# Naming the PSUM bank of each feed-forward tile and re-ordering a fused attention and feed-forward kernel

## The chip, the cores and the metric

The kernel runs on one core of one Trainium2 chip. The metric is the device time of one execution in microseconds. The kernel before has a median of 408.99 us over three runs (408.08, 413.05 and 408.99).

Five engines take part. TensorE (PE) multiplies matrices and writes only to PSUM, an accumulator memory of eight banks. VectorE (DVE) and ScalarE (ACT) read PSUM and write SBUF, the working memory. GpSimd (POOL) works in SBUF and issues some DMA transfers. SyncE (SP) issues most transfers. Each engine takes its own instructions strictly in the order in which the program emits them, and engines wait for one another through semaphores.

## The reference

Eight batches of eight heads attend over 576 positions of 64 values, with a decay between positions that comes from a running sum of the logarithm of `f`. The result, 4608 tokens of 512 values, goes through a feed-forward layer with two input matrices that are multiplied element by element.

```python
scores = scale * np.matmul(q, k.transpose(0, 1, 3, 2))
cum = np.cumsum(np.log(np.clip(f, 0.0001, 1.0)), axis=-1)
decay = cum[:, :, :, None] - cum[:, :, None, :]
scores = np.where(causal, -1000000000.0, scores + decay)
attn = softmax(scores)                       # with 1e-09 added to the sum
x = np.matmul(attn, v)  -> reshaped to (4608, 512)
out = ((x @ w_a) * (x @ w_b)) @ w_out        # w_a, w_b: 512 x 1536; w_out: 1536 x 512
```

## The kernel before

Attention works on 32 steps t, each a pair of heads of one batch (four steps to a batch). One step goes through these operations; their names are those of the planner and are used below.

- `pt` transposes a quarter of a batch's queries or keys on TensorE into a PSUM tile `psT`; `pe` evicts that on ACT or DVE.
- `qk t.g` computes the scores of one group g of query blocks into a PSUM tile `sc` of two banks; there are two such tiles. Group 0 is the pair of blocks 0 and 1. From batch 1 on, the `max` operations on DVE add the decay from the table `spread`, write the sum to SBUF, and find the row maximum (`do_decay`, L575). In batch 0 the decay is added on TensorE.
- `exp` on ACT (L602, L606), a reciprocal on DVE (L614, L616), `norm` on POOL (L624).
- `tr` transposes the probabilities by DMA on SP's queue; the early steps use TensorE instead (`ptr`, L74) and evict with `pev`.
- `pv` multiplies the probabilities by the values (L666, L682); `ev` copies the result to the layer's input `xT`.

From batch 2 on, `pv` of step t-2 is emitted with step t. Its last part, `do_pv4` for the 64 queries left over, writes to columns 448 to 511 of the first bank of step t's group 0 score tile, which the scores leave unused ("spare"). So two unrelated values share a bank: the scores of step t, which DVE reads four times (`max t.0` and `max t.1`, two heads each), and the older step's output, which L693 reads.

The feed-forward layer takes tokens in pieces of 256, 256, 256, 384 and then 512. For each piece and each of twelve blocks of the hidden dimension, TensorE makes `psa` and `psb` (eight matmuls each), ACT copies `psa` (`acopy`), DVE multiplies it by `psb` (`mul`, L964), and three groups of eight matmuls per 128 tokens make `pso`, which ACT or DVE copies out (`ocopy`) and SP stores. This layer's work is spread between the attention steps, so that TensorE has something to do while DVE, ACT and POOL work on the softmax; a last part remains when attention is done.

Six kinds of PSUM tile share three banks under the tag "ff": `psT`, `scd` (which spreads the decay table), `psP` (of `ptr`), `psa`, `psb` and `pso`. The tile pool of the program gives each new tile one of the three (`bufs=3`), as they come free in the order of emission. There are 396 such tiles.

The emission order is fixed: each piece of work is an `Op` with an engine, a duration, the operations that it depends on, and the buffers it takes. A planner outside the kernel uses these to look for an order; the kernel holds its answer, a list of 2460 operation numbers (`ORDER`), and a letter for each operation that may run on several engines (`CHOICE`, 103 letters). `laid_out` reads both, and the operations are emitted in that order. The framework adds the semaphore waits that the emitted order needs: a reader waits for the writers emitted before it, and a writer for the readers emitted before it.

Of the kernel before, what the change touches and what calls it, by code (L numbers as in the profile page):

```python
# [25 lines left out]
def kernel(  # L26
# [111 lines left out]
    ps = pool("ps", 1, space=bass.MemoryType.PSUM)  # L138
    VEC = {"ACT": nc.scalar, "DVE": nc.vector, "POOL": nc.gpsimd}
# [29 lines left out]
    T = {}  # L169
# [132 lines left out]
    def pe_transpose(b, which, half):  # L302

        x = T[("n16", which, b, half)]
        x = x if b in EARLY else x.rearrange("p t h d -> p t (h d)")
        p = [ps.tile([128, 1024], FP16, tag="ff", bufs=3, name="psT") for _ in range(2)]
        for t in range(TG):
            for j in range(2 if b in EARLY else 1):
                for m, r in enumerate(HP):
                    nc.tensor.matmul(out=p[m][HP[j] if b in EARLY else slice(0, 128), 64 * t:64 * t + 64],  # L310
                                     lhsT=x[r, j, t, :] if b in EARLY else x[r, t, :], rhs=ident16[r, r],
                                     is_transpose=True, start=(t == 0), stop=(t == TG - 1), skip_group_check=True)
        for m in range(2):
            T[("psT", which, b, 2 * half + m)] = p[m]
# [201 lines left out]
    def spread_mm(t, h):  # L516
        c = T[("scd", t, h)] = ps.tile([128, 512], FP32, tag="ff", bufs=3, name="scd")
# [122 lines left out]
    def pe_tr(t, part, lo, hi):  # L640
        src = PB[t % RING["PB"]] if part == "B" else T[("P", part[0], t)]
        p = ps.tile([128, 8, 128], FP16, tag="ff", bufs=3, name="psP")
# [70 lines left out]
    def attention(t, base):  # L713
# [36 lines left out]
        qk_of, sc_of = {}, {}  # L750
        qk_prev = None
        for gs in ([(0,), (1,), (2, 3)] if b in EARLY else [(0,), (1,), (2,), (3,)]):
# [30 lines left out]
            if gs == (0,) and b not in EARLY and old // NP not in EARLY:  # L783
# [166 lines left out]
    def ff_mm(t0, n, fb, w16, name):  # L950
        p = ps.tile([128, 512], FP32, tag="ff", bufs=3, name=name)
# [16 lines left out]
    def ff_out(t0, tb, part):  # L968
        if part == 0:
            T[("pso", t0, tb)] = ps.tile([128, 512], FP32, tag="ff", bufs=3, name="pso")  # L970
# [98 lines left out]
    for n in cuts:  # L1069
# [3 lines left out]
        0-2 45 49 53 28-31 36 32 37-39 33 35 41 34 4-9 46 10 47 50 43 51 52 11 57 3 78 54 56 65 63 61 42  # L1073
# [5 lines left out]
        101 106 23 24 162 244 163 245 207 387 263 208 252 125 264 265 107 253 102 388 144 1750-1752 150  # L1079
# [15 lines left out]
        461 460 379 448 1827 1831 455 443 1832-1834 1836 1838 465 466 1835 472 1802 512 498 514 377 429  # L1095
        1807 467 1837 517 1840-1842 432 1844 473 1839 1843 468 1845 474 1846 1848 521 433 1849 499 449
        513 515 564 456 522 462-464 450 524 380 1850 1852 520 523 1847 529 469 530 470 381 475 543 544
# [7 lines left out]
        606 621 620 589 485 694-696 608 486 1902 1904 1903 1906 627 1907 1908 632 633 1905 578 705 585  # L1105
# [10 lines left out]
        759 904-906 798 772 813 1977-1979 749 717 735 908 820 742 766 801 769 802 1980 811 761 760 821  # L1116
        793 804 803 741 787 788 795 912 914 856 857 1976 1982 817 909 1983 1984 910 823 835 836 828 805
        807 806 915 799 911 822 1987 819 838 830 837 839 842 843 1988 1985 1989 1991 1992 824 1993 1990
        829 1994 841 794 800 812 840 763 762 1981 1995 818 916 814 831 825 779-781 832 928 827 834 929
# [5 lines left out]
        934 921 935 936 2029 924 923 933 962 922 949 2031-2033 2035 2036 2030 953 2034 954 1112 1020  # L1125
# [113 lines left out]
```

## Time and profile before

| quantity | value |
|---|---|
| median of three runs | 408.99 us (408.08 to 413.05) |
| the profiled execution | 408.72 us, of which the span from first to last instruction is 407.0 us |
| TensorE busy | 392.3 us (96% of the span), 5792 matmuls |
| VectorE busy | 303.6 us (75%) |
| ScalarE busy | 280.1 us (69%) |
| GpSimd busy | 263.0 us (65%) |
| mean granted TensorE clock | 0.996 |

The busy time of an engine is the time in which at least one of its instructions was running. A row of a timeline has the start and the length of an instruction or of a merged run of like instructions, with "xN" for their count, and in brackets the idle time of the engine before it and the event that ended that idle time. A row of the waits names who waited for whom, the total in microseconds, how often, and the longest. Idle time of an engine that does not set the pace costs nothing by itself.

### The profile page before, as it was taken

Reading aid. Unit: us, or ns where it says so; the run is one execution under the profiler, and the core shown is the slowest. Engines: PE = TensorE matmul, PEld = TensorE weight load, DVE = VectorE, ACT = ScalarE, POOL = GpSimd, SP = SyncE. Lnnn points to the kernel's source line nnn. Section 1 sums busy time; section 2 is a strip of 40 time slices with the busy share of each in tenths; the row PEclk is TensorE's granted clock in tenths of the full one; section 3 lists DMA queues with packets and bytes.
Section 4 is the critical chain, followed back from the end, with each engine's and each line's share of the span. In section 5 each row is a group of like instructions: output and inputs, shape, how many; then the busy total and the mean of one; then the engine's idle time right before and its main releaser. Section 6 shows DMA issues by size and latency. Waiting matters only on the chain. (4 is left out here: it accounts for less than half of the span.)

```text
span 407.0 us, 14850 instructions
## 1 busy us (share of the span) xinstructions
PE 392.3 (96%) x5792; PEld 246.9 (61%) x5792; DVE 303.6 (75%) x1012; ACT 280.1 (69%) x793; POOL 263.0 (65%) x488
## 2 busy tenths in 40 slices
PE   7899799999999999999999899999999999999995
PEld 2557586877966655555556456555555555556783
DVE  4888788999898888977896989679878884432331
ACT  4698799979986688787785678488676882231230
POOL 8898569868888588686987774778975493000000
PEclk9899999999999999999999999999999999999999
DMA  7999996999999999999999989999998569100202
GB/s 127 188 208 161 183 217 158 216 282 209 270 266 215 222 228 235 262 254 216 259 212 271 260 194 240 234 262 256 192 199 187 111 137 183 53 2 22 86 2 77
DMA packets 147190, 76.88 MB, mean 189 GB/s; under 512 B 124336, under 2 KB 129200, under 8 KB 147120
## 3 DMA queue, kind: packets, MB, share of 16 engines
q1 hardware_dynamic: 141040, 68.73, 75.3%
q0 software_dynamic: 5936, 7.08, 10.8%
q8 instruction: 45, 0.74, 0.7%
q14 instruction: 25, 0.20, 0.2%
q10 hardware_dynamic: 144, 0.13, 0.1%
HBM read 52.05 MB, written 9.58 MB: 151 GB/s over the span
## 5 line engine op out<-in xcount | busy, mean ns | idle before, releaser
L575 DVE CUSTOM_DVE_ANT_0 S<-sc,spread 64x576 f32<-64x576 f32 (+4 forms) x232 | 125.8, 562 | 11.3 <-PE sc L682 3.2
L74 PE MATMUL psb<-xT,wb 128*64 128x512 f16 (+2 forms) x1056 | 117.4, 341 | 1.4 <-DMA wb<-in_moe_w_b_dram 1.0
L74 PE MATMUL psa<-xT,wa 128*64 128x512 f16 (+2 forms) x1056 | 117.4, 341 | 0.4 <-issue 0.2
L624 POOL TENSOR_SCALAR PA<-PA,st 128x256 f16<-128x256 f16 (+2 forms) x192 | 90.2, 480 | 35.0 <-DVE st L616 23.6
L258 ACT CAST a<-psa 128x512 f16<-128x512 f32 (+2 forms) x132 | 66.6, 505 | 62.0 <-PE psa L74 54.0
L964 DVE TENSOR_TENSOR ht<-psb,a 128x512 f16<-128x512 f32 (+2 forms) x132 | 77.4, 590 | 33.5 <-PE psb L74 29.0
L74 PE MATMUL pso<-wout,ht 128*64 128x512 f16 x864 | 101.4, 380 | 0.0
L606 ACT ACTIVATE PA<-S,st 128x256 f16<-128x256 f32 (+2 forms) x168 | 84.3, 504 | 13.3 <-DVE st L575 12.9
L624 POOL TENSOR_SCALAR PB<-PB,st 128x512 f16<-128x512 f16 (+1 forms) x96 | 67.6, 712 | 18.6 <-DVE st L616 4.6
L74 PEld LDWEIGHTS <-wb 128*64 128x64 f16 x1056 | 60.3, 110 | 31.6 <-issue 3.4
L74 PEld LDWEIGHTS <-wa 128*64 128x64 f16 x1056 | 60.1, 110 | 31.2 <-issue 2.5
L74 PEld LDWEIGHTS <-ht 128*64 128x64 f16 x864 | 48.8, 110 | 35.4 <-issue 1.3
L606 ACT ACTIVATE PB<-S,st 128x512 f16<-128x512 f32 x56 | 40.2, 720 | 4.1 <-DVE st L575 3.5
L452 PE MATMUL sc<-kT,qT 64*128 64x128 f16 (+3 forms) x384 | 34.1, 267 | 1.3 <-ACT qT L256 0.4
L606 ACT ACTIVATION_READ_ACCUMULATOR PA<-S,st 128x1 f32 x168 | 32.0, 190 | 0.0
L262 DVE CAST xT<-pv 128x512 f16<-128x512 f32 (+1 forms) x40 | 23.1, 577 | 6.4 <-PE pv L666 6.2
L262 DVE COPY osb<-pso 128x512 f32<-128x512 f32 x17 | 11.7, 689 | 19.9 <-PE pso L74 19.8
L452 PEld LDWEIGHTS <-qT 64*128 64x128 f16 (+1 forms) x384 | 13.2, 95 | 21.7 <-issue 14.5
L666 PEld LDWEIGHTS <-nv 128*64 128x64 f16 x640 | 22.4, 110 | 6.5 <-issue 1.3
L602 ACT ACTIVATE PB<-S,st 128x576 f16<-128x576 f32 x28 | 21.8, 778 | 5.9 <-POOL PA L624 2.3
L575 DVE CUSTOM_DVE_ANT_1 S<-sc,spread 128x256 f32<-128x256 f32 x48 | 19.8, 418 | 7.7 <-PE sc L682 2.4
L258 ACT COPY osb<-pso 128x512 f32<-128x512 f32 x18 | 10.4, 580 | 20.7 <-DMA out_dram<-osb 10.8
(101 smaller groups left out, 480.9 us busy)
## 6 DMA issues: line engine op xcount, KB each, us to landing
spread<-cum_d SPq DMA_DIRECT2D x24, 576.0 KB, 5.8
out_dram<-osb SPq DMA_DIRECT2D x35, 256.0 KB, 3.5
v<-in_v_dram SPq DMA_DIRECT2D x32, 256.0 KB, 5.3
q<-in_q_dram SPq DMA_DIRECT2D x12, 576.0 KB, 6.0
k<-in_k_dram SPq DMA_DIRECT2D x12, 576.0 KB, 6.5
wout<-in_moe_w_out_dram POOLq DMA_DIRECT2D x3, 512.0 KB, 7.6
v<-in_v_dram SPq DMA_DIRECT2D x8, 128.0 KB, 3.7
wb<-in_moe_w_b_dram POOLq DMA_DIRECT2D x2, 512.0 KB, 9.9
```

Of the source, the lines that this page charges most:

```text
L74: nc.tensor.matmul(out=out[r], lhsT=lhsT[:, r], rhs=rhs, **kw)
L258: nc.scalar.copy(out=out_, in_=in_)
L262: VEC[e].tensor_copy(out=out_, in_=in_)
L452: nc.tensor.matmul(out=dst, lhsT=lhsT, rhs=rhs, start=start, stop=stop, skip_group_check=True)
L575: nc.vector.tensor_tensor_reduce(out=o, in0=x, in1=y, scale=-1.0, scalar=3e38, op0=ADD, op1=MIN, accum_out=m)
L602: nc.scalar.activation(out=p_blocks(t, 4), in_=T[("s" if direct else "z", t, 4)], func=EXP, bias=st[:, 8:9], scale=sign, accum_out=st[:, 1 ...
L606: nc.scalar.activation(out=p_blocks(t, i)[:, :, h, :], in_=(T[("s", t, i)][:, h, :] if direct else T[("z", t, i)][:, h * n:h * n + n]).rea ...
L624: VEC[e].tensor_scalar(out=p, in0=p, scalar1=st[:, c:c + 1], scalar2=1.0, op0=MUL, op1=MUL)
L666: nc.tensor.matmul(out=o[HP[h], 128 * i:128 * i + 128], lhsT=vt[:, j, pr + NP * h, :], rhs=pt[:, base_blk[i] + 2 * block_at(t, i, j) + h, ...
L964: nc.vector.tensor_tensor(out=ht[:, 0:n], in0=T.pop(("psb", t0, fb))[:, 0:n], in1=T.pop(("a16", t0, fb))[:, 0:n], op=MUL)
```

## The change

Three things change in the text of the kernel.

1. The six places that took a tile from the pool of three buffers now call `ff_tile`, which takes the next digit of a table `FFBANK` (396 digits, 0 to 2) and asks for the one buffer under that tag. The tiles, their count and their contents are as before.
2. In the operations' dependencies, `pv` of step t-2 gets the four `max` operations of step t's group 0 as predecessors, so in any order that the planner finds it is emitted behind them.
3. `ORDER` and `CHOICE` are replaced by new ones.

The operations themselves, the number of matmuls (5792) and the buffers are the same.

```diff
+    ff_bank = []
+
+    def ff_tile(shape, dtype, name):
+        return ps.tile(shape, dtype, tag=f"ff{ff_bank.pop(0)}", bufs=1, name=name)
...
-        p = [ps.tile([128, 1024], FP16, tag="ff", bufs=3, name="psT") for _ in range(2)]
+        p = [ff_tile([128, 1024], FP16, "psT") for _ in range(2)]
...
-        p = ps.tile([128, 512], FP32, tag="ff", bufs=3, name=name)
+        p = ff_tile([128, 512], FP32, name)
...
-        qk_of, sc_of = {}, {}
+        qk_of, sc_of, spare_pv = {}, {}, []
...
                 sc_of[0].append(pv)
+                spare_pv.append(pv)
                 late[old][1](pv, sc_of[0])
...
+                    if g == 0 and spare_pv:
+                        spare_pv[0].deps.append(mx)
...
     ORDER = """
-        0-2 45 49 53 28-31 36 32 37-39 33 35 41 34 4-9 46 10 47 50 43 51 52 11 57 3 78 54 56 65 63 61 42
...
+        0 1 45 2 49 28 29 4-8 46 9 10 30-33 36 37 47 48 50 51 35 38 34 39 11 53 57 3 78 61 65 63 42 54
...
     CHOICE = """
-        DDPDADAADADDPADDDDDAADDADDADDDADAAAAAADDAADADADADADAADAAAAAAAADAAAAADADAAADAAADAAAAADDADDADD
-        ADAAAAAAADA
+        DDDPAAAADADAPPADADDDADDADDADDAAAAADAAADDADDDADDAADAAAAAAAAADAAAAAAAADAAAAADAAAAAAAAADAAAAADA
+        DAADAAAAADA
     """
+    FFBANK = """
+        02102101201021021021012012012012012012012012021012021021021210210210212012021021012012012012
...
     def laid_out():
+        ff_bank.extend("".join(FFBANK.split()))
```

Compared operation by operation, the new order keeps the broad course of the old one. On TensorE the steps' score groups, the feed-forward groups and the `pv` stand in nearly the same sequence from end to end; neighbours are exchanged. Before, in six of the 22 late `pv` (those of steps 8, 15, 19, 22, 26 and 27) one to three of the four readers of the shared bank were emitted behind the `pv`; after, none. On POOL the first load of keys stands ahead of the identity matrix that TensorE's first matmuls need, where it stood behind it; the last input weights (`ldwa`, `ldwb`) no longer stand behind a part of `w_out`, and the load `ldc1q1` stands ahead of the last of them. Seven evictions of transposed queries and keys move from DVE to ACT, one copy of the decay table moves from DVE to ACT, and one cast of values from DVE to POOL.

More of the change, by code (lines that the diff above doesn't have):

```diff
@@ L516, in spread_mm @@
     def spread_mm(t, h):
-        c = T[("scd", t, h)] = ps.tile([128, 512], FP32, tag="ff", bufs=3, name="scd")
+        c = T[("scd", t, h)] = ff_tile([128, 512], FP32, "scd")
         mm_halves(c, pickh[h][:, t:t + 1].to_broadcast([128, 128]), crow[:, 0:512], start=True, stop=True)
@@ L641, in pe_tr @@
         src = PB[t % RING["PB"]] if part == "B" else T[("P", part[0], t)]
-        p = ps.tile([128, 8, 128], FP16, tag="ff", bufs=3, name="psP")
+        p = ff_tile([128, 8, 128], FP16, "psP")
         for n in range(lo, hi):
@@ L969, in ff_out @@
         if part == 0:
-            T[("pso", t0, tb)] = ps.tile([128, 512], FP32, tag="ff", bufs=3, name="pso")
+            T[("pso", t0, tb)] = ff_tile([128, 512], FP32, "pso")
         o = T[("pso", t0, tb)]
@@ L1105 @@
-        606 621 620 589 485 694-696 608 486 1902 1904 1903 1906 627 1907 1908 632 633 1905 578 705 585
[10 rows of a table removed]
[L1116 to L1119, printed above, removed]
[5 rows of a table removed]
@@ L1125 @@
-        934 921 935 936 2029 924 923 933 962 922 949 2031-2033 2035 2036 2030 953 2034 954 1112 1020
[9 rows of a table removed]
-        1061 2078-2080 1080 1086 2081 1075 2083 2084 1094 1093 2085 2082 1098 1099 2086 1088 1139 1051
[4 rows of a table removed]
-        1142 1131 1146 1153 1144 1140 1143 1159 2106 1172 1187 1175 1177 1133 1194 1323 2108-2110 1160
-        1195 1197 1132 1176 1178 2111 1111 1110 2113 1191 1329 2114 1188 2107 1240 1135 1167 1203 1161
-        1179 1162 1173 1202 1154 1169 1168 1181 1196 1209 1174 1210 1204-1206 1189 1330 1331 1198 1211
[10 rows of a table removed]
@@ L1153 @@
-        1272 1275 1261 1253 1274 1292 1299 1533 1307 1317 1319 1312 1537 2172 1374 1360-1362 1367 1363
-        2173 1376 1375 1318 1404 1306 1293 1357 2176-2178 2181 1352 2182 1380 2179 1366 2174 1368 1381
[8 rows of a table removed]
-        1475 2218-2220 1499 1493 2221 2223 1544 1558 1549 1418 1463 1481 1445 2222 1511 1512 1469 1559
-        1500 1550 1476 1464 1543 1482 1471 1456 1457 1483 2224 1439 1438 2225 2227 1514 2228 1513 1507
-        1504 2226 1501 1502 1506 1494 1551 1490 2229 1552 1492 2190 1604 1556 1485 2185 1495 1515 1508
@@ L1166 @@
-        2230 1518 1519 2231 2232 1553 2233 2235-2237 1517 1516 1503 1488 1470 1484 1545 1510 1491 1523
-        1520 2234 1524 1521 2238 1525 1526 2239 2240 1561 1546 1565 2241 1527 1569 1583 1584 1548 1547
-        1571 1586 1577 1585 2242 1587 1570 1572 1579 2244 1567 2245 1562 2246 2249 1564 1576 1573
-        1590-1592 1578 1563 2250 1566 1607 2251 1509 1605 1650 1522 1614 1528 1529 1660 1575 1651 1560
[8 rows of a table removed]
-        2294 1726 1693 1721 1720 1722 1723 1681 1655 1714 1715 1692 1716 2295-2297 1709 2298 1732 1733
[4 rows of a table removed]
@@ L1183 @@
-        2341 2340 2342 2343 2345 2344 2347 2349 1749 2346 2348 2351-2353 2350 2354 2355 2357 2356 2358
-        2359 2361 2360 2362-2365 2367-2370 2366 1698 2371 2373 2372 2375 2376 1706 1699 2374 2377
-        2380-2383 2385-2387 2390 2391 2378 2384 2379 2388 2392 2395 2397 2396 2399 2393 2398 2389 2394
-        2401 2400 2403 2402 2405 2404 2407 2409 2408 2406 2410 2411 2413 2412 2415 2417 2416 2414 2419
-        2421 2420 2418 2423 2425 2424 2422 2426 2427 2429 2428 2430 2431 2433 2432 2435 2437 2436 2434
@@ L1188 @@
-        2439 2441 2440 2438 2442-2445 2448 2446 2449 2450 2453 2451 2454-2456 2447 2452 2457-2459
+        0 1 45 2 49 28 29 4-8 46 9 10 30-33 36 37 47 48 50 51 35 38 34 39 11 53 57 3 78 61 65 63 42 54
[6 rows of a table added]
+        104 272 233 72 142 103 386 1750-1752 145 1753 201 202 150 1754-1757 108 25 146 151 1758 387 1760
[9 rows of a table added]
+        339 438 368 361 362 494-496 314 315 320 505 488 500 1803 1804 373 1805 506 360 489 497 363 364
[6 rows of a table added]
+        529 530 520 1846-1848 1850 524 474 380 513 471 457 464 1852 532 1849 523 1851 1807 510 543 544
[4 rows of a table added]
@@ new lines @@
+        603 554 547 553 601 588 692 555 1878-1880 1882 1884 556 559 591 611 1881 1883 613 1886 1888 1887
[12 rows of a table added]
+        777 1968-1970 773 1972 1973 1971 791 792 1974 785 1975 796 723 782 784 797 793 776 798 748 908
[5 rows of a table added]
+        851 833 834 827 920 826 846 938 869 2000 2002 839-841 2004 2005 875 2006 865 2007 884 870 883
+        2009 860 2008 877 876 888 889 862 2011 2012 890 926 912 974 864 931 2013 852 858 853 871 873 929
+        2015 885 861 2010 893 878 2014 894 2016 895 2017 891 896 2018 939 941 940 2019-2021 937 946 947
[10 rows of a table added]
@@ new lines @@
+        1042 1044 1043 1091 1092 2075 1079 2076 2077 1094 1093 2074 2078 1078 1075 2079-2081 2083 1080
[5 rows of a table added]
+        1090 1172-1174 1140 1102 1155 2105 2106 1165 2108 1142 1144 1146 1131 1187 1175 1167 1176 1195
+        1143 1132 1177 1178 1133 2049 1230 1322 2109-2111 2113 1191 1329 2114 2115 1202 1179 1209 1210
[3 rows of a table added]
+        1241 1219 1248 2126 1224 1225 2127 2129 2131 1255 2128 1243 1257 1242 1256 2132-2134 2130 1258
[7 rows of a table added]
+        2168 1351 1355 2169-2172 2122 1274 1275 2117 1359 2173 1307 1533 1361 1360 1373 1375 1366 1367
[8 rows of a table added]
@@ new lines @@
+        1559 1444 2211-2213 2215 1462 1455 1464 1487 1470 1471 2214 1463 1457 1456 1496 1446 1474 2216
[8 rows of a table added]
+        1638 1624 2252 2254 2255 1608 2256 1610-1612 1609 1599 1629 1626 2257 2259 2261 2260 1631 2263
[5 rows of a table added]
+        1725 1712 1713 2288 2291 1719 1726 1721 1728 2292 1718 1665 2290 1685 1709 2293-2295 2297 1720
[3 rows of a table added]
+        1696 2317-2319 1697 1743 1742 1736 1744 1745 2311 2322 2323 1746 2324 1747 2315 2320 2321 1698
+        2327 2328 1699 2325 1706 2316 2329 2326 2330-2333 2335 2337 2336 2334 2338 2339 1748 2340 2341
@@ L1189 @@
+        1749 2342-2349 2351-2353 2350 2354-2369 2371-2373 2375 2376 2374 2370 2377 2380-2383 2385-2387
[3 rows of a table added]
+        2442-2445 2448 2446 2449 2450 2453 2451 2454-2456 2452 2447 2457-2459
     """
     CHOICE = """
-        DDPDADAADADDPADDDDDAADDADDADDDADAAAAAADDAADADADADADAADAAAAAAAADAAAAADADAAADAAADAAAAADDADDADD
-        ADAAAAAAADA
+        DDDPAAAADADAPPADADDDADDADDADDAAAAADAAADDADDDADDAADAAAAAAAAADAAAAAAAADAAAAADAAAAAAAAADAAAAADA
+        DAADAAAAADA
+    """
+    FFBANK = """
+        02102101201021021021012012012012012012012012021021021021210210210212012021021012012012012012
+        01202102012012102102101201201201201201201201201012012012021012012021021021201212021021012012
+        02102012012102120120121202012010201202102012012102102101020212102101021201201202102012012012
+        01012120120120120120102101202102100210210212012012021021021021021201201201201201201201201012
+        1021021021021021021021021021
```

4 lines of the change are left out of this document (removed), and 179 rows, old and new, of the table ORDER.

## The prediction

> **What bounds the kernel now.** I read the page first, then busy time by stretches, then the waits.
>
> ```profile
> span 407.0 us, 14850 instructions
> PE 392.3 (96%) x5792; PEld 246.9 (61%) x5792; DVE 303.6 (75%) x1012; ACT 280.1 (69%) x793; POOL 263.0 (65%) x488
> PE   7899799999999999999999899999999999999995
> DVE  4888788999898888977896989679878884432331
> ```
>
> TensorE is busy in nearly every slice. DVE is dense until about slice 33 and has time to spare in the last seven, where only feed-forward work is left. So TensorE is the bound, and another engine costs time only where TensorE ends up waiting for it. How much can be won is what TensorE stands idle (columns: stretch, length, PE busy with its matmuls, weight loads, DVE, ACT, POOL, granted clock, DMA):
>
> ```profile
> 0.00:20.00 20.00, 15.90 (x268) 7.95 (x269) 12.87 (x27) 11.74 (x33) 16.75 (x49) 0.91 0.92 157
> 20.00:60.00 40.00, 37.14 (x810) 27.25 (x807) 34.16 (x103) 34.07 (x107) 30.27 (x54) 1.00 1.07 190
> 60.00:220.00 160.00, 158.77 (x2526) 104.81 (x2522) 137.52 (x502) 130.92 (x374) 128.00 (x226) 1.00 1.05 237
> 220.00:280.00 60.00, 57.81 (x774) 33.07 (x772) 47.88 (x168) 42.41 (x122) 42.81 (x78) 1.00 1.04 230
> 280.00:400.00 120.00, 119.81 (x1408) 72.23 (x1404) 70.07 (x214) 60.59 (x162) 45.15 (x85) 1.00 0.51 116
> 400.00:407.00 7.00, 2.91 (x28) 1.57 (x24) 1.12 (x2) 0.37 (x1) 0.00 (x0) 1.00 0.21 75
> ```
>
> Length less PE busy: 4.10 us idle in the first 20 us (inputs are awaited), 2.86, 1.23, 2.19 and 0.19 in the four stretches between, 4.09 at the end (copy and store of the last tile). The edges hold 8.2 us that no bank and no order of the middle touches; 20 to 400 us holds 6.47 us. The waits name most of this (waiting line, releaser, total us, times, longest):
>
> ```profile
> DVE S L575 <- PE sc L682: 5.6, 3, 2.4
> PE sc L74 <- DVE st L575: 1.3, 1, 1.3
> PE psb L74 <- DMA wb<-in_moe_w_b_dram: 1.0, 1, 1.0
> PE sc L682 <- DVE st L575: 0.8, 2, 0.6
> PE psT L310 <- DVE xT L262: 0.5, 1, 0.5
> ```
>
> The first row is the one that the new dependency aims at: DVE, about to read scores, waits for an older step's matmuls into the spare columns of the same tile.
>
> **The shared bank.** The largest case, in order of time:
>
> ```profile
> 222.07 0.34 PE L452 MATMUL sc<-kT,qT 64*128 64x128 f16 x4
> 224.05 0.32 PE L682 MATMUL sc<-PTB,nv 128*64 128x64 f16 x10
> 224.41 0.29 DVE L575 CUSTOM_DVE_ANT_0 S<-sc,spread 128x128 f32<-128x128 f32 x1 [2.33 <-PE sc L682]
> 226.49 0.41 PE L74 MATMUL sc<-kT,qd 128*64 128x512 f16 x2 [1.26 <-DVE st L575]
> ```
>
> At 222.07 `qk21.1` is issued; group 0 of step 21 had been there for some microseconds. DVE stands 2.33 us until `pv19` has written the spare columns at 224.05. It then reads the blocks late, the score buffer comes free late, and TensorE stands 1.26 us before the next group at 226.49. The two other cases:
>
> ```profile
> 184.96 0.42 DVE L575 CUSTOM_DVE_ANT_1 S<-sc,spread 128x256 f32<-128x256 f32 x1 [2.38 <-PE sc L682]
> 186.58 0.39 PE L452 MATMUL sc<-kT,qT 64*128 64x512 f16 x2
> 263.38 0.29 DVE L575 CUSTOM_DVE_ANT_0 S<-sc,spread 128x128 f32<-128x128 f32 x1 [0.89 <-PE sc L682]
> 264.54 0.60 PE L452 MATMUL sc<-kT,qT 64*128 64x512 f16 x8 [0.34 <-DVE st L575]
> ```
>
> Of these the first leaves no gap at TensorE's next score group (186.58, no idle time in brackets), the other one of 0.34 us. With all 22 late `pv` emitted behind their four readers, DVE cannot wait for them any more. Gain: 1.26 + 0.34 = 1.6 us on TensorE. The upper end is the whole 5.6 us of DVE, if each came through; the lower end is below nothing, since the wait changes sides: now TensorE, at its matmuls into the spare columns, waits for DVE. The trace has that already where `pv` stood behind the readers:
>
> ```profile
> 131.18 0.35 PE L682 MATMUL sc<-PTB,nv 128*64 128x64 f16 x10 [0.60 <-DVE st L575]
> ```
>
> Everything on TensorE queues behind it: the next feed-forward groups, and with them `acopy` and `mul`. Before, 16 `pv` were in this position and cost 0.8 us in two waits. How near are the 22 of the new order? I counted, from the end of `qk t.0` to `pv`, TensorE's work against DVE's from the first to the last of the four reads. The nearest is `pv24`: two short score groups (about 0.5 us) and four feed-forward groups, each 0.86 us by the second row below from the chain of waits, 3.9 us in all; DVE has in that time two reads of 256 columns, two of 384, two of 128, two products and three reciprocals.
>
> ```profile
> 224.63 0.16 DVE L616 RECIPROCAL st<-st 128x2 f32<-128x2 f32 x1
> 224.96 0.42 DVE L575 CUSTOM_DVE_ANT_1 S<-sc,spread 128x256 f32<-128x256 f32 x1
> 225.31 0.55 DVE L575 CUSTOM_DVE_ANT_0 S<-sc,spread 128x384 f32<-128x384 f32 x1
> 215.01 0.69 DVE L964 TENSOR_TENSOR ht<-psb,a 128x512 f16<-128x512 f32 x1 [1.27 <-ACT a L258]
> ```
>
> ```profile
> 229.78 0.98 PE pso L74 x8
> 230.76 0.86 PE psa L74 x8
> ```
>
> With 0.29 for a read of 128 that is 0.84 + 1.10 + 0.58 + 1.38 + 0.48 = 4.4 us: a wait of about 0.5 us. The others have half a microsecond or more to spare, which the old `pv10` (131.18) had not. So I leave this row at 0.8 us, and take **-1.6** for the part, from -5.6 to +3 (0.6 for each of five more).
>
> **The bank table.** The tile pool already gave banks out of strict rotation, as they came free. From the last matmul that fills a tile to the first that reuses its bank, TensorE's own work is under 0.9 us for 43 of the reuses before and 42 after, and never under 0.4. The cover, two other tiles' matmuls at 0.86 us a group against an eviction by `acopy` or `mul` (0.69 above), is the same. Cost **0**; if a bank is named that comes free late, one eviction, 0.69 us a place, shows as a gap on TensorE. No wait of before is put down to such a place above 0.3 us.
>
> **The loads on POOL.** At about 47 us TensorE waited 0.99 us for the last part of `w_b`, and soon after 0.54 us at the transposes of the last queries of batch 1, whose load also came late:
>
> ```profile
> 34.55 0.80 POOL L427 DMA_DIRECT2D wout<-in_moe_w_out_dram  x1
> 35.34 0.63 POOL L427 DMA_DIRECT2D wa<-in_moe_w_a_dram  x1
> 35.95 0.64 POOL L427 DMA_DIRECT2D wb<-in_moe_w_b_dram  x1
> 38.63 0.75 POOL L289 DMA_DIRECT2D q<-in_q_dram  x1
> 48.61 0.63 PE L74 MATMUL psb<-xT,wb 128*64 128x256 f16 x8 [0.99 <-DMA wb<-in_moe_w_b_dram]
> ```
>
> That `w_b` was issued third of three, 12 us before it was used. In the new order no part of `w_out` stands ahead of it, `w_b` goes ahead of the last `w_a`, and the `q` load ahead of that. The needs on TensorE stay where they were (the fifth `psa` and `psb`). All of them landing in time gives 1.5 us; the last `w_a` being now the late one takes 1.0 back, and the second key load of batch 1, which now stands behind more `norm` work on POOL, could cost as much. I take **-1.0**, from -1.5 to +1.0.
>
> **The start.** The identity now stands behind one load, which holds POOL for 0.91 us:
>
> ```profile
> 1.09 0.29 POOL masks.py:199 TENSOR_SCALAR_AFFINE_SELECT ident<-ident 128x128 f16<-128x128 f16 x1
> 1.51 0.91 POOL L289 DMA_DIRECT2D k<-in_k_dram  x1
> 1.44 5.45 PE L74 MATMUL wake<-ident 128*64 128x512 f16 x24 [1.44 <-POOL ident masks.py:199]
> 8.71 0.48 PE L310 MATMUL psT<-ident,q 64*64 64x64 f16 x36 [0.79 <-DMA q<-in_q_dram]
> 11.87:15.28 3.41, 3.26 (x60) 2.07 (x61) 2.58 (x7) 2.26 (x9) 1.60 (x7) 0.50 1.26 244
> ```
>
> The first matmuls ("wake") come 0.9 us later, but they only fill time until the keys and queries land; the query load, which is awaited at 8.71, is issued when it was. Cost **0**, from -0.7 (keys earlier) to +0.9 (wakes still running), apart from the clock, below.
>
> **The rest of the order.** Moves of evictions from DVE to ACT take nine copies off DVE and put eight on ACT; both hide behind TensorE. A feed-forward group that follows scores takes 0.98 instead of 0.86 us (the two rows of the chain above); such changes are nearly as many in both orders: nothing to 0.3 us less, 0.1 taken. The unnamed gaps of the middle (6.47 less the 1.6, 1.5 and 0.8 above, 2.6 us) will be others of the same kind: **0**, from -2.6 to +5. Counted with the trace's durations, 316 us of TensorE's work stand ahead of attention's last score group in both orders, so the part behind it is as long as it was.
>
> **Sum.** 408.72 - 1.6 - 1.0 - 0.1 = 406.0 us for an execution like the profiled one, which lies 0.3 us under the median of 408.99.
>
> **Rivals.**
>
> *Given back elsewhere.* DVE's waits go and TensorE meets others, so that the table and the new order do nothing that can be seen. For it: the wait of 2.38 us on DVE left no gap, so what DVE gains need not reach TensorE; and the banks were already taken as they came free. Against it: the 1.26 us did come through. 408 to 410.
>
> *TensorE takes the wait (slower).* The place is the first matmul into the spare columns, the price 0.6 us each time, and it decides as soon as DVE runs half a microsecond later than my count at most `pv`: DVE is busy 137.5 of 160 us, so one late table or one late exponential moves several reads. 22 x 0.6 = 13.2 us; with the rest of the forecast 406 + 13 = 419; half of it, 413. Against it: only two of 16 waited. The Trainium skill's page "PSUM — Partial Sum Buffer", section "PSUM bank collisions raise a hardware error", speaks for this rival: it asks to guard PSUM by bank and quadrant and not by address, so reads and writes of different columns may not overlap whoever goes first. By that rule the wait cannot vanish, only move, and here it moves to the engine that sets the pace; the 2.33 us above, with columns that do not overlap, agrees.
>
> *The clock.* For 3.41 us from 11.87 the granted clock was 0.50, after gaps of TensorE at 8 to 11 us; this costs half of it, 1.7 us, in a run. With the wakes 0.9 us later another such stretch could come, at +1.7 us: 407.7, or 408.6 with the 0.9; or this one could go, at 404.3. The skill's page "TensorE: Matmul & The Clock Gate", Part 1, says that the clock rises only after a busy window of about 3.4 us in a free-running count. By that rule a later first matmul can miss a window; the length of 3.41 us here agrees.
>
> *All gaps of the middle close.* DVE, ahead by 5.6 us, never makes TensorE wait: 408.7 - 6.5 = 402.2. Against it: new orders bring gaps of their own.
>
> **How the numbers follow.** Chances: the forecast (404.3 to 407.5) 0.42; given back or a clock stretch more (to 411) 0.30; all gaps close (400.5 to 404) 0.13; TensorE takes the wait, in part or wholly (411 to 419) 0.15. The likeliest gives 406.0. From 401.5 to 413 leaves out some 0.05 below and 0.08 above. Two per cent, 8.2 us, is about what a measurement of this kernel tells from no change, its own three runs lying 5 us apart: under 400.8 needs more than every gap of the middle, 0.05; over 417.2 needs most of the slower rival, 0.07; within, 0.88.
>
> **What would show it.** Right: no wait of DVE's L575 on L682; L682 waiting for DVE about 0.8 us in all; no 0.99 us gap at `w_b`; TensorE idle between 20 and 400 us about 4 us. Wrong: L682 waiting more than 3 us in all; gaps at 30 to 50 us for `k` or `w_a`; a first clock stretch at 0.50 longer than 3.41 us.

## The result and the profile after

The changed kernel takes 406.29 us (median of 20 runs, 404.19 to 410.11); the kernel before, run beside it on the same chip, 410.42 us (20 runs, 408.08 to 413.05). The ratio is 0.9908, 95% interval 0.9886 to 0.9930: 2.9 to 4.7 us less. In a second measurement, beside the experiments, it was 0.9930 (0.9906 to 0.9955). The profiled execution took 406.14 us, of which the span is 404.4; before, 408.72 and 407.0.

The page of the changed kernel, the rows that answer to those of before:

```profile
span 404.4 us, 14858 instructions
PE 389.1 (96%) x5792; PEld 240.6 (60%) x5792; DVE 298.2 (74%) x1003; ACT 283.6 (70%) x801; POOL 262.3 (65%) x489
PE   6899799999999999999999997999999999999995
DVE  3777888999888888876897786788979882541331
```

The shares have hardly moved: TensorE is still the bound, at 96%. Of the 2.6 us between the two profiled spans, about 1.7 are the stretch at half clock that the execution of before had near 12 us (half of 3.41 us) and this one had not; the size of the gain is therefore read from the medians. The page also shows a 7 in TensorE's row at slice 25, which is looked at below. Busy time by stretches, in the columns that the prediction explains:

```profile
0.00:20.00 20.00, 14.84 (x278) 7.32 (x278) 11.71 (x27) 12.49 (x35) 17.32 (x51) 1.00 1.02 179
20.00:60.00 40.00, 36.47 (x810) 27.47 (x806) 32.59 (x101) 34.09 (x107) 30.49 (x54) 1.00 0.95 174
60.00:220.00 160.00, 159.79 (x2537) 104.45 (x2532) 137.63 (x503) 133.22 (x380) 129.81 (x231) 1.00 1.09 243
220.00:280.00 60.00, 57.84 (x806) 33.13 (x804) 47.57 (x172) 44.83 (x129) 41.46 (x74) 1.00 1.06 229
280.00:400.00 120.00, 119.82 (x1382) 68.28 (x1378) 68.31 (x204) 58.62 (x153) 43.25 (x83) 1.00 0.51 109
400.00:404.40 4.40, 0.34 (x4) 0.00 (x0) 0.42 (x1) 0.37 (x1) 0.00 (x0) 1.00 0.34 122
```

Length less PE busy gives TensorE's idle time: 5.16, 3.53, 0.21, 2.16, 0.18 and 4.06 us. Before it was 4.10, 2.86, 1.23, 2.19, 0.19 and 4.09. So the start holds a microsecond more of idle time, 20 to 60 us 0.7 more, 60 to 220 us 1.0 less, and 220 to 280 us looks as before. Two of these figures mislead. At the start the clock was 1.00 here and 0.91 before, so that the same matmuls fill less time: by count, matmul 300 starts at 22.48 us here and at 22.73 before. And 220 to 280 us hides a gap of this one execution, as the waits and the gaps of TensorE show. First the waits (waiting line, releaser, total us, times, longest): the one that is left between DVE and the spare columns, and TensorE's four longest:

```profile
DVE xT L698 <- PE sc L687: 6.4, 9, 3.0
...
PE wake L74 <- POOL ident masks.py:199: 2.9, 1, 2.9
...
PE pv L671 <- DMA PTB<-PB: 2.1, 1, 2.1
PE psa L74 <- DVE qT L265: 1.3, 1, 1.3
PE pv L671 <- issue: 1.2, 1, 1.2
```

Then the three largest gaps behind the start, in the timeline:

```profile
44.50 0.25 PE L671 MATMUL pv<-xT,nv 128*64 128x128 f16 x2 [1.21 <-issue]
50.28 0.63 PE L74 MATMUL psa<-xT,wa 128*64 128x256 f16 x8 [1.33 <-DVE qT L265]
246.45 0.25 PE L671 MATMUL pv<-PTB,nv 128*64 128x128 f16 x2 [2.06 <-DMA PTB<-PB]
```

Lines have moved: the decay read is L580 (L575 before), the matmuls into the spare columns are L687 (L682), and the copy that reads them is L698 (L693). DVE's 5.6 us at the decay read for older steps' matmuls are gone: there is no such row any more. The row of L698 is not the same thing; it is the copy that has to wait for its own matmuls. Its row was 2.3 us in six waits before and is 5.0 us in ten in the profile of the second measurement, so part of DVE's waiting has moved there; no wait of TensorE's is put down to it. Nor is there a row in which L687 waits for DVE. In 220 to 280 us the whole 2.06 us belong to one late transpose of probabilities, in this one execution: in the profile of the second measurement the same stretch holds 0.11 us of idle time. And at 44.5 and 50.3 us there are two gaps that before had not, or not in this size (0.46 us at the first place). The first has no releaser at all; the second is put down to DVE's eviction of the queries, of which more below.

### The profile page after: what moved, and what is told of

It reads as the page before. It is cut to its first block, busy times and chain, and to the rows that moved or that the text cites. A ratio compares the mean times of both kernels' runs of the same rounds, so it can differ in the third digit from the quotient of the medians.

```text
span 404.4 us, 14858 instructions
## 1 busy us (share of the span) xinstructions
PE 389.1 (96%) x5792; PEld 240.6 (60%) x5792; DVE 298.2 (74%) x1003; ACT 283.6 (70%) x801; POOL 262.3 (65%) x489
## 4 chain that ended last, share of the span: by engine, by line
PE 65%; DMA 3%; DVE 2%; ACT 0%; issue 0%; ACTq 0%; DVEq 0%
PE pso L74 19%; PE psa L74 18%; PE psb L74 18%; PE sc L457 4%; PE pv L671 3%; DMA PTB<-PB 2%; PE sc L74 1%; PE psT L315 1%; DMA out_dram<-osb 1%; DVE S L580 1%; PE sc L687 1%; DVE osb L267 0%; DVE ht L972 0%; ACT osb L263 0%; DVE half L267 0%
## 5 line engine op out<-in xcount | busy, mean ns | idle before, releaser
L580 DVE CUSTOM_DVE_ANT_0 S<-sc,spread 64x576 f32<-64x576 f32 (+4 forms) x232 | 125.4, 562 | 14.0 <-PE sc L457 4.0
L629 POOL TENSOR_SCALAR PA<-PA,st 128x128 f16<-128x128 f16 (+2 forms) x192 | 89.8, 478 | 24.8 <-DVE st L621 16.0
L74 PEld LDWEIGHTS <-wa 128*64 128x64 f16 x1056 | 58.3, 110 | 35.6 <-issue 4.5
L74 PEld LDWEIGHTS <-wb 128*64 128x64 f16 x1056 | 58.0, 110 | 31.6 <-issue 1.9
L74 PEld LDWEIGHTS <-ht 128*64 128x64 f16 x864 | 47.0, 110 | 37.5 <-issue 1.0
L457 PE MATMUL sc<-kT,qT 64*128 64x128 f16 (+4 forms) x384 | 33.8, 266 | 1.5 <-ACT qT L261 1.1
L580 DVE CUSTOM_DVE_ANT_1 S<-sc,spread 128x256 f32<-128x256 f32 x48 | 19.7, 419 | 5.3 <-PE sc L457 2.2
L580 DVE DVE_READ_ACCUMULATOR2_ANT st<- 128x1 f32 (+1 forms) x280 | 22.9, 82 | 0.0
```

The lines of the kernel that those rows point to most:

```text
L74: nc.tensor.matmul(out=out[r], lhsT=lhsT[:, r], rhs=rhs, **kw)
L457: nc.tensor.matmul(out=dst, lhsT=lhsT, rhs=rhs, start=start, stop=stop, skip_group_check=True)
L580: nc.vector.tensor_tensor_reduce(out=o, in0=x, in1=y, scale=-1.0, scalar=3e38, op0=ADD, op1=MIN, accum_out=m)
L629: VEC[e].tensor_scalar(out=p, in0=p, scalar1=st[:, c:c + 1], scalar2=1.0, op0=MUL, op1=MUL)
```

## The experiments

### Three waits turned, nothing else

TensorE's, DVE's and every other engine's order and every bank stay as in the kernel before; only the emission of three `pv` changes, so that three waits change sides (a `pso` group of TensorE that follows `pv22` moves along with it; " ..." stands for other operations between, among them two more of the readers at `pv19`):

```diff
-pv15 PE
 ...
 max17.1 DVE
+pv15 PE
...
-pv19 PE
 ...
 max21.1 DVE
+pv19 PE
...
-pv22 PE
 ...
 max24.0 DVE
+pv22 PE
```

> The kernel before with every engine's own instructions in the same order and every tile in the same bank; only the emission of three older values (pv of steps 15, 19 and 22) is put behind the four readers of the bank they share, so three waits change sides. Theory that these waits made TensorE late: DVE no longer stands 2.4, 2.3 and 0.9 us for L682 (it keeps the short ones of steps 8, 26 and 27), and 1.6 to 3 us go, a ratio of 0.993 to 0.996. Rival, that the gain comes from the order as a whole and DVE's loss was covered: ratio 0.999 to 1.001.

Measured: 407.23 us, ratio 0.9937 (0.9911 to 0.9963), 1.5 to 3.6 us less. The timeline of this kernel where before had the 2.33 us wait of DVE and the 1.26 us gap of TensorE:

```profile
223.51 0.27 DVE L575 CUSTOM_DVE_ANT_0 S<-sc,spread 128x128 f32<-128x128 f32 x1
...
224.04 0.42 DVE L575 CUSTOM_DVE_ANT_1 S<-sc,spread 128x256 f32<-128x256 f32 x1
...
225.56 0.32 PE L682 MATMUL sc<-PTB,nv 128*64 128x64 f16 x10
...
226.58 0.41 PE L74 MATMUL sc<-kT,qd 128*64 128x512 f16 x4
```

DVE reads without a wait, and the last of the four reads of this bank (block 1, 256 columns) ends at 224.46; TensorE comes to the spare columns at 225.56, 1.1 us later, and waits for nothing either; the next score group follows with no gap. The dependency stands, but here nobody pays for it. So the turned waits alone give most, or all, of what the whole change gives.

### One wait, and the two others

The first of the three (`pv15`, 2.38 us on DVE, no gap at TensorE's next score group) alone, and the other two alone:

```diff
-pv15 PE
 ...
 max17.1 DVE
+pv15 PE
```

> The kernel before with only pv15 emitted behind the readers of the bank that it shares; the order of every engine and every bank are as before, so one of DVE's three waits goes, the 2.38 us one that left no gap at TensorE's next score group. My prediction's step: it is worth nothing, ratio 0.999 to 1.001, and the gain of the three (ratio 0.9937) comes from the other two. Rival (what DVE loses arrives at TensorE later, in gaps that name another releaser): the ratio is 0.994 to 0.997, at least half of 2.38 us.

Measured: 409.00 us, ratio 1.0001 (0.9971 to 1.0031). The waits of this kernel show the two others still there:

```profile
DVE S L575 <- PE sc L682: 3.2, 2, 2.3
...
PE sc L74 <- DVE st L575: 1.3, 1, 1.3
...
PE sc L452 <- DVE st L575: 0.3, 1, 0.3
```

```diff
-pv19 PE
 ...
 max21.1 DVE
+pv19 PE
...
-pv22 PE
 ...
 max24.0 DVE
+pv22 PE
```

> The kernel before with only pv19 and pv22 emitted behind the readers of the bank that they share; the order of every engine is as before. My prediction's step: their waits had let 1.26 and 0.34 us through to TensorE, so 1.6 us less, ratio 0.996. Rival (the traces with all three turned: between the same matmuls 1.45, 0.34 and 0.30 us less, the last in a gap that named another releaser): 2.1 us less, ratio 0.995. With the wait of pv15 worth nothing, the ratio of all three, 0.9937, should be met within its interval (0.9911 to 0.9963); a ratio above 0.998 would mean that pv15 and these two only count together.

Measured: 407.02 us, ratio 0.9930 (0.9901 to 0.9960), 1.6 to 4.1 us less. The two waits whose gaps could be seen at TensorE carry the gain, and the one without a gap is worth at most 1.2 us by the interval. In these kernels TensorE executes the same matmuls in the same order, so the time between the starts of two matmuls, counted from the first, compares them without the scatter of the start (us, worked out from the traces):

| matmuls | before | loads only (below) | `pv15` | `pv19`, `pv22` | all three |
|---|---|---|---|---|---|
| 3000 to 3300 (`pv15`) | 23.08 | 23.07 | 22.65 | 23.07 | 22.76 |
| 3600 to 3700 (`pv19`) | 7.73 | 7.73 | 7.73 | 6.28 | 6.28 |
| 3700 to 4300 (`pv22`) | 45.06 | 45.04 | 45.03 | 43.94 | 44.43 |
| 4300 to 4500 | 17.79 | 17.78 | 17.41 | 17.42 | 17.41 |
| 2300 to 4500, all of it | 166.61 | 166.52 | 165.73 | 163.63 | 163.84 |

`pv19` is worth 1.45 us, `pv22` 0.6 to 1.1, `pv15` 0.3 to 0.4. The 0.4 us behind matmul 4300 went with any of them; why is open.

### Waits turned back

In the changed kernel, `pv` emitted ahead of as many readers as the other dependencies allow, at eleven steps by the order of emission; the engines' orders stay. One of them:

```diff
-max13.1 DVE
 ...
 pv11 PE
+max13.1 DVE
```

> The changed kernel with every engine's own order and every bank as they are, but the older values emitted ahead of as many readers of their bank as the order allows (one to four of the four readers, at ten steps). Theory of the shared bank: DVE waits for L687 again at some of them, 2 to 5 us in all, and 1 to 3 us of the gain go, a ratio to the kernel before of 0.993 to 0.999. Rival, order as a whole: the ratio stays at 0.991.

Measured: 437.76 us, ratio 1.067 (1.062 to 1.072), some 31 us slower than the changed kernel: far outside what I had written. Its waits:

```profile
DVE S L580 <- PE sc L687: 27.6, 10, 3.9
...
PE psT L315 <- DVE ht L972: 6.5, 7, 2.8
PE sc L457 <- DVE st L580: 6.0, 4, 3.1
...
PE psa L74 <- DVE ht L972: 3.1, 3, 1.1
```

DVE loses 27.6 us in ten waits. TensorE stands idle for 34.3 us of the profiled span, 19 to 20 more than in the two traces of the changed kernel, not only at the scores (6.0) but at transposes and feed-forward groups that wait for `mul`, which stands behind the waiting reads on DVE. The idle time costs a second time: this trace has four stretches at half clock, 17.1 us in all, each behind 3.41 us in which TensorE stood for 1.9 to 2.7 us; half of that, 8.5 us, is the estimate of what they cost. The changed kernel's two traces have none before their end. I had taken the price from the three waits of before, one of which was worth 0.3 to 0.4 us; it does not carry over to others.

### The bank table

The six places take their tile from one tag with three buffers again, in the changed kernel; 260 of the 396 tiles then lie in another bank, the orders are the same:

```diff
     def ff_tile(shape, dtype, name):
-        return ps.tile(shape, dtype, tag=f"ff{ff_bank.pop(0)}", bufs=1, name=name)
+        return ps.tile(shape, dtype, tag="ff", bufs=3, name=name)
```

> The changed kernel with the table taken out: the pool gives the banks as they come free, and 260 of the 396 tiles land in another bank; each engine's order is the same. My forecast cost the table at nothing: ratio 0.991 to the kernel before, as the changed kernel. Rival, that naming the banks is what brings the gain: 0.995 to 1.000, with TensorE waiting for ACT or DVE at psa, psb or pso.

Measured: 405.22 us, ratio 0.9912 (0.9885 to 0.9938). The changed kernel itself, run beside it:

> The changed kernel again, beside the other three on the same chip: 0.989 to 0.993. The 2.06 us wait of TensorE for a transposed block near 246 us and the 1.2 and 1.3 us gaps near 44 and 50 us are there again if they belong to the order, and gone or elsewhere if they were of that one execution.

Measured: 406.17 us, ratio 0.9930 (0.9906 to 0.9955). The table is worth nothing that can be measured; the intervals leave room for a microsecond or two.

### The loads alone

```diff
+ldc1q1 POOL
+ldwb POOL
+ldwa POOL
 ldwo POOL
-ldwa POOL
-ldwb POOL
...
-ldc1q1 POOL
```

> The kernel before with nothing changed but POOL's order of four loads: the last queries of batch 1, then the last part of w_b, then the last part of w_a, then the part of w_out (before: w_out, w_a, w_b, and the queries later). All other engines keep their order. My prediction's term: the 0.99 us gap at w_b and the 0.54 us gap at the query transposes go, 1.0 to 1.5 us less, ratio 0.9963 to 0.9976 to before. Rival (instruction fetch): TensorE gets no instructions in time at the ends of blocks of 256 instructions, which fall at matmuls 734 and 862 (44 and 50 us) in every kernel; the two gaps only gave the fetches time. Then the two gaps go and unnamed gaps of 0.5 to 1.5 us stand at matmuls 734 and 862, and the ratio is 0.998 to 1.002.

Measured: 409.21 us, ratio 0.9997 (0.9971 to 1.0023). All gaps of TensorE between 40 and 56 us in this kernel's timeline, and its row of busy time for 20 to 60 us:

```profile
42.45 0.25 PE L666 MATMUL pv<-xT,nv 128*64 128x128 f16 x2 [0.29 <-issue]
49.35 0.26 PE L310 MATMUL psT<-ident,q 64*64 64x64 f16 x9 [1.86 <-issue]
```

```profile
20.00:60.00 40.00, 37.26 (x800) 27.74 (x796) 33.04 (x102) 33.14 (x101) 29.25 (x51) 0.96 1.05 185
```

The 0.99 us at `w_b` and the 0.54 us at the queries are gone. But TensorE is idle 2.74 us in the stretch (2.86 before), since a gap of 1.86 us without a releaser has opened at 49.35. The rival was right on the places and on the ratio; the interval, -1.2 to +0.9 us, does not quite exclude the -1.0.

That the loads closed the two gaps is not shown either, for the gaps differ between executions with the same loads. In the traces of the three and of the two turned waits, whose loads stand as before, there is no wait for `w_b`: the gap without a releaser ahead of it is 1.1 to 1.2 us instead of 0.46, and `w_b` has landed by then. With `pv15` alone the wait for `w_b` is 0.52 us, and the stretch holds 4.28 us of idle time, 1.4 more than before with the same orders there. So the 0.7 us that the changed kernel has more than before lies within what one execution differs from another.

### What the gaps without a releaser are

TensorE's instructions come by a DMA queue of their own. The page's row of that queue, and the same row for the stretch from 41.85 to 42.90 us, ahead of the gap at 44.5 (both of the changed kernel):

```profile
q8 instruction: 45, 0.74, 0.8%
```

```profile
q8 instruction: 1, 0.02, 5.7%
```

0.74 MB in 45 packets are 16 KB each; 45 blocks of 256 instructions are 11520, and TensorE has 5792 matmuls and as many weight loads, 11584. Counted in the trace from zero, the gap of the changed kernel without a releaser stands at matmul 734, the misnamed one at 862, and smaller ones at 479 and 990: 128 matmuls, with their 128 weight loads 256 instructions, apart, or about twice that. Between 20 and 60 us every kernel of this study has its gaps without a releaser at some or all of 479, 734, 861 or 862, and 989 or 990, in differing size. Where a gap opens, the packet ahead of it had begun 2.2 to 2.9 us before the first matmul behind the gap. To tell that from a cause in the operations themselves, I shifted the blocks under the program, in the changed kernel:

```diff
-    def wake(n):
+    def wake(n, cols=512):
...
-    ... lambda _: wake(2), [o_i], ...
+    ... lambda _, n=n: (wake(1), wake(21, 64)) if n == 6 else wake(2), [o_i], ...
```

> The changed kernel with one warm-up step (between the transposes of the first keys and queries, where TensorE waits anyway) sending 2 matmuls of 512 columns and 42 of 64 instead of 4 of 512: 40 more matmuls in about the same time, so every block of 256 instructions ends 40 matmuls earlier in the program. Fetch theory: the gaps stay at matmuls 734 and 862 by count, but these are now other operations of the program, with longer work ahead of them; from about 2.4 us between fetch and use and the durations of the changed kernel's trace, 1.2 and 1.3 us become 0.2 to 0.4 each, other block ends gain up to 0.5, and the time is 1 to 2 us less than the changed kernel's (ratio 0.987 to 0.990 to before). Rival (the gaps belong to these operations: an operand or a buffer that no row names): gaps of 1.2 and 1.3 us at the same operations as before, then matmuls 774 and 902 by count, and the time is that of the changed kernel (0.991 to 0.995).

Measured: 407.71 us, ratio 0.9963 (0.9935 to 0.9992). All its gaps from 38 to 60 us (the rows with brackets), and the two operations that follow the first of them:

```profile
48.88 0.30 PE L672 MATMUL pv<-PTB,nv 128*64 128x128 f16 x4 [1.57 <-issue]
49.11 0.48 PE L316 MATMUL psT<-ident,q 64*64 64x64 f16 x36
49.52 0.63 PE L74 MATMUL psa<-xT,wa 128*64 128x256 f16 x8
...
55.08 0.20 PE L458 MATMUL sc<-neg,low 64*128 64x64 f16 x2 [1.71 <-issue]
```

These are matmuls 862 and 990 by count, now other operations; at 774 and 902, where the old operations have gone, is no gap, and at 734 none either. The `psa` at 49.52 is the one that stood 1.33 us in the changed kernel, put down to DVE's eviction of the queries; here it follows their transposes at once, so it had not waited for that eviction. The gaps belong to the block ends, and the place of the theory held. Its sizes did not, nor its time: I had taken each fetch to begin some 45 matmuls ahead of the block's end, and here the two began 20 and 12 ahead, and the ratio, 0.9963, lies above both forecasts, though its interval reaches into the rival's. How far ahead a fetch begins I could not foresee from the traces.

### The start undone

```diff
 ldf1 SP
+ident POOL
 ldc0k0 POOL
-ident POOL
```

> The changed kernel with the identity matrix ahead of the first key load again, as before; nothing else. My prediction's term for the start: nothing, so the same ratio to before as the changed kernel's, 0.991 to 0.995. Rival (the clock): the late first matmul decides whether TensorE falls back to half clock at 8 to 15 us; then a stretch at 0.50 returns and the time is 1.0 to 1.7 us more than that of the changed kernel (ratio 0.996 to 0.999).

Measured: 406.54 us, ratio 0.9935 (0.9903 to 0.9966). The time is that of the changed kernel, and the profiled execution had a clock of 1.000 throughout. The other executions say more. One stretch of 3.41 us at half clock takes the mean granted clock of an execution to 0.996. A mean of 0.998 or more stands in 25 of the 74 executions of the kernel before on which the ratios of the experiments rest (on average 0.9959), in 18 of the 29 of the changed kernel (0.9979), and in 2 of these 9 (0.9948). So the order at the start seems to go with how often the clock falls, and the time does not show it. A reason can be estimated: with the early identity matmul 300 starts at 21.88 us in this trace, against 22.48 and 22.64 in the two of the changed kernel, so the undone start may gain at first what it loses by the clock. Nine executions do not settle it.

Stretches at half clock come later too: the traces of the loads alone, of the two turned waits and of the three each have one that begins 0.3 to 1.6 us behind a gap of 1.8 to 1.9 us at matmul 861 (the row of the loads above, with 0.96).

### Late warm-up steps left out

Eight of the 24 warm-up steps stand between useful work from 23 to 41 us. Without them, and without the last three only:

```diff
-    ... lambda _: wake(2), [o_i], ...
+    ... lambda _, n=n: n >= 16 or wake(2), [o_i], ...
```

> The changed kernel without the last eight of its 24 warm-up steps, 32 matmuls that stand between useful work from 23 to 41 us (about 0.44 us a step, 3.5 us in all); the output does not depend on them. Theory A (TensorE's own work is the bound there, what follows is ready): 2.5 to 3.5 us less than the changed kernel, ratio 0.983 to 0.987 to before. Theory B (instruction fetch bounds 40 to 56 us: a block of 256 instructions is usable about 2.4 us after its fetch starts, and shorter work between only lengthens the gaps at matmuls 734, 862 and 990 by count): unnamed gaps grow at these counts by 1 to 2 us together, and half or more of the 3.5 us is given back, ratio 0.988 to 0.993. Clock theory: a stretch at half clock comes in, ratio above 0.993.

Measured: 404.85 us, ratio 0.9885 (0.9846 to 0.9923). Its waits:

```profile
PE psb L74 <- issue: 1.4, 1, 1.4
PE psT L315 <- DVE spread L267: 1.3, 1, 1.3
...
PE sc L457 <- DVE st L619: 0.8, 1, 0.8
...
PE psP L74 <- issue: 0.6, 1, 0.6
PE psP L74 <- POOL PA L629: 0.6, 1, 0.6
```

```diff
-    ... lambda _: wake(2), [o_i], ...
+    ... lambda _, n=n: n >= 21 or wake(2), [o_i], ...
```

> The changed kernel without the last three warm-up steps, 12 matmuls at 36 to 41 us (1.3 us). Theory A (own work bounds): 1.0 to 1.3 us less than the changed kernel, ratio 0.988 to 0.990 to before. Theory B (instruction fetch): 0 to 0.5 us less, ratio 0.990 to 0.994, with unnamed gaps at matmuls 734 and 862 of 2.5 us or more together.

Measured: 404.05 us, ratio 0.9856 (0.9816 to 0.9896). Its waits:

```profile
PE psT L315 <- issue: 1.0, 1, 1.0
PE psP L74 <- issue: 0.9, 1, 0.9
PE psa L74 <- issue: 0.9, 1, 0.9
PE sc L457 <- DVE st L619: 0.8, 1, 0.8
```

> The changed kernel without its last three warm-up steps a second time, since 404.05 us (ratio 0.9856) was about 2 us less than the changed kernel's, more than the 1.3 us of work left out, of which its trace gives 0.8 us back in a new gap. If leaving them out is worth its traced net, 0.3 to 0.5 us, the ratio is 0.988 to 0.992, within the intervals of the changed kernel (0.9908 and 0.993); if it is worth 2 us, 0.984 to 0.987 again.

Measured: 404.83 us, ratio 0.9887 (0.9840 to 0.9933). With eight steps out, 3.5 us of work make room for 2.7 us of waits with names (1.3, 0.8, 0.6): the steps had stood where inputs were not ready. The unnamed gaps at matmuls 734 and 862 (0.6 and 1.4) are not longer than in the changed kernel (1.2 and 1.3). So the time fits the second theory but not its reason. With three out, 0.8 of 1.3 us come back the same way, and the unnamed gaps (1.0, 0.9, 0.9) are again at block ends, 479, 734 and 990 by count. At 404 to 405 us this is the fastest version of the study. Its first interval lies below the second of the changed kernel (0.9906 to 0.9955) and overlaps the first, its second overlaps both, and its trace accounts for only half a microsecond. That it beats the changed kernel is likely and not shown.

## Why the prediction was right, and where it was not

406.0 us was forecast, 406.29 measured. That the two agree so closely is in part luck. The forecast took 2.7 us off a profiled execution of 408.72; measured on one chip, the change took 4.1 us off 410.42 (2.9 to 4.7 by the interval). Two of the terms were off in opposite directions, and a third effect, the clock, was counted at nothing.

- **The shared bank, -1.6:** the mechanism was right, and the size too small. "Gain: 1.26 + 0.34 = 1.6 us" counted the gaps that named DVE's late reads. The two waits gave 1.6 to 4.1 us, and between matmuls 2300 and 4500 of the traces 3.0 us; what lay beyond the named gaps (0.3 to 0.8 us behind `pv22`, 0.4 behind matmul 4300) came as shorter gaps and denser groups that no row puts down to the reads. The step that the 2.38 us "left no gap" and so were worth nothing held within the interval; 0.4 us of it arrived.
- **The wait that changes sides, "I leave this row at 0.8 us":** there is no such wait in the changed kernel. My count of 4.4 us of reads against 3.9 us of TensorE's work for `pv24` was too careful, though `pv24` was rightly picked as the nearest: in the changed kernel's trace DVE takes 3.5 us from the start of the first of the four reads (275.07) to the end of the last (278.60), as each instruction begins some 0.07 us before the one ahead of it ends, and TensorE arrives at 279.23, 0.63 us later. The rival in which TensorE takes the wait is out. The Trainium skill's page "PSUM — Partial Sum Buffer", section "PSUM bank collisions raise a hardware error", has the rule to guard a bank by semaphores and not by address. This case does not contradict it: the order is there, and the timeline of the three turned waits shows it met 1.1 us early. What does not follow from it is the prediction's step that the wait "cannot vanish, only move".
- **The bank table, 0:** right as far as 0.9912 and 0.9930 side by side can tell.
- **The loads on POOL, -1.0:** the step that failed. "All of them landing in time gives 1.5 us" took for granted that nothing else was late at 44 to 50 us. In the trace of the loads alone the gaps went, as said, and TensorE then waited for its own instructions: the ratio was 0.9997, -0.1 us, with -1.0 just inside the interval (-1.2 to +0.9). The two gaps are also closed, or smaller, in traces with the old loads, so they were not there to be won in every execution. The bounds named the late `w_a` and the second key load; neither came late.
- **The start, 0, and the clock:** the time agrees, the reason is open. Undone, the start left the time as it was. But the changed kernel's executions ran at a higher mean clock than those of before (0.9979 against 0.9959, an estimated 0.8 us of 407), and with the start undone it was 0.9948 again; so a part of the whole gain probably is the stretch that "could go", the prediction's own rival. Among the executions with a clock of 0.998 or more the medians are 408.43 us (25 of before) and 406.16 (18 of the changed kernel), 2.3 us apart. The Trainium skill's page "TensorE: Matmul & The Clock Gate", Part 1, says that the clock's window of activity runs free and does not begin with the kernel, so a first matmul 1.4 us later can meet it differently. No run here shows whether that decides it.
- **The rest of the order, -0.1:** the three turned waits alone give 0.9937 and the whole change 0.9908 and 0.9930, with overlapping intervals. Nothing is left over that can be told from zero, and the clock could account for the difference.
- **"TensorE idle between 20 and 400 us about 4 us":** 6.08 us, of which 2.06 are the one late transpose of this execution, and 5.52 in the second profile, which does not have it. So this sign missed: less was lost at the scores, and about as much as before, or more, to instruction fetch.

"Given back elsewhere" was half true: in the one trace of the loads alone, what they gained was given back within 2 us of the same place.

## What to carry to other kernels

When two unrelated values share a bank, look at which of the two engines comes first in time, and emit in that order: in this kernel the same dependency cost up to 2.4 us of DVE's time a place one way, and nothing of TensorE's at any of the 22 places in the new order. Price a wait by its effect on the bound engine and add what follows it there, for the named gaps were about half of it here; and where two gaps a few microseconds apart have different causes, ask what the second cause needs before counting the first as won. Look at the clocks of all executions, not only of the profiled one, before calling the clock unchanged. Filler work between useful work is not free until one has looked at what it covers.

## What was new of the hardware

TensorE can starve for instructions. In these runs they come in packets of 16 KB, each for 256 instructions (128 matmuls and their weight loads). Between 20 and 60 us, where the matmuls come densest (810 in 40 us, against 2537 in the next 160), TensorE stood 0.2 to 2.8 us at the ends of these blocks and went on 2.2 to 2.9 us behind the start of the packet. The gaps stand at the same count of matmuls whatever the program has there, some without a releaser and some put down to one that was not awaited. What decides when a packet is asked for stays open.

The clock fell without a long gap. All eleven stretches at half clock in the traces of this study, apart from those at the very end of a span, followed 3.41 us in which TensorE stood idle for 1.5 to 2.7 us in all, in one gap or in several. Not every such idle time was followed by one: behind the longest gap of all, 2.79 us, the clock stayed at 1.00.
